# Lightning attention and a leaky-ReLU feed-forward block: heads kept in memory order, k and q of a chunk in one transfer each, w_in rows loaded in two parts

## The chip, the cores and the metric

The kernel runs on one core of one Trainium2 chip. Its time is the device time in microseconds of that core. Several runs of the same program are made and the median is given; a separate execution is recorded by the hardware profiler, and all rows below come from that one execution. Five engines work side by side: PE (matrix multiplication, with PEld for its weight loads), DVE (vector), ACT (scalar), POOL and SP, which in this kernel issues nearly all DMA transfers. Each engine runs its own instructions in a fixed order and waits for others through semaphores.

## What is computed

```
q, k, v: (4, 8, 768, 64) float32      # batch, heads, sequence, head size
w_in: (512, 2048), w_out: (2048, 512) # both float64
for b in range(12):                   # blocks of 64 positions
    intra = einsum('bhic,bhjc->bhij', qb, kb) * Dmask       # lam_h ** (i - j), lower triangle
    intra = einsum('bhij,bhjd->bhid', intra, vb)
    inter = einsum('bhid,bhde->bhie', qb * lam_pow, kv_state)
    out[:, :, sl] = intra + inter
    kv_state = lam_block * kv_state + einsum('bhsd,bhse->bhde', kb * rev_pow, vb)
x = out.transpose(0, 2, 1, 3).reshape(3072, 512)            # head h is columns 64h to 64h + 63
h = x @ w_in
g = maximum(0.01 * h, h)
result = g @ w_out                                          # (3072, 512) float32
```

The feed-forward products need more accuracy than one pass of the fast matrix format gives, so the kernel splits each factor into parts.

## The kernel before

**Tiling.** The 3072 tokens are 24 chunks of 128 (six per batch element, `NCB`), each of two blocks of 64; four chunks make a group of 512 tokens. A chunk of attention handles all eight heads together. Its result goes into the tiles `xh`, `xl`, `xm` with the 512 columns of `x` on partitions, as four row blocks of 128: two heads to a block, one in the lower 64 partitions and one in the upper. The up product multiplies these by slices of `w_in` of 256 columns (eight slices `p`), each held as three parts `wh`, `wl`, `wm`; the results pass the leaky ReLU (ACT, L883) and are stored in DRAM. When all groups are up, the down product runs over them with `w_out` prepared in the meantime. The attention of later groups is worked in between the up products of earlier ones.

**A chunk of attention.** `load_kq` (L455) and `load_v` (L525) bring k, q and v with the 128 positions on partitions and eight heads side by side. `load_kq` issues two transfers for k and two for q: heads 0, 2, 4, 6 go to the first four places of the tile, heads 1, 3, 5, 7 to the last four. `transposes` (PE, L550) turns two adjacent places at a time; copies to SBUF follow (L531 on ACT or DVE, L598 for the scaled q). From chunk 8 for q and chunk 10 for k the turned form is loaded instead by many small transfers (L513, `load_subs`, 32 partitions each) and finished by DVE. `scores` (L613) makes the products of k and v for the state (`kv`) and those of k and q (`go`); DVE multiplies the latter by the decay mask (L643) and adds to the state (L650), and POOL decays it (L653). `outputs` (L658) sums `own` (scores by v) and `inter` (state by q, in two halves, with a tiny copy L682 between them on DVE or ACT that the second half waits for) in the PSUM tile `po`. L698, L706 and L724 split the result into `xh`, `xl`, `xm`.

All small products go through `quad` (L409): a 64 × 64 weight block in one of four quadrants of the PE array, chosen by the row half (which 64 partitions the factors lie in) and the column half (which 64 output partitions). `place` (L416) tells where the scores and the state of head number `h`, in memory order, lie: heads are numbered in the tile order even-then-odd there, so that output half `hi` of row block `y` is head `2y + hi`.

**Decay factors.** `factors` (L378) copies the broadcast `lam` with the even heads first into `lam_h`; `factors_k` (L382) builds an identity-like tile `eye` (L383) and scans each head's powers (L386); `factors_q` (L389) does the same for q (L391, L393). All on DVE, in this order.

**w_in.** `w_in(p)` loads a slice in two halves `h` (L787): row blocks `2h` and `2h + 1` of 128 rows and 256 columns of float64, that is 128 partitions with two pieces of 2 KB. `to_float32` (L770) makes float32 from the bits with three ACT instructions (L799, L801, L803) and two of DVE (L805, L806); `parts` (L808) makes `wh`, `wm`, `wl` (L813 to L820). Three `raw` tiles hold the loads; one of them also takes the q of chunk 3, and the `gs` tiles take k and v of chunks 2 and 3.

**Order.** A planner (`Plan`, L45) emits the instructions. For the start and most of the up phase the order is not computed but taken from a list written out by hand (`ORDER`, L266), pairs of an operation's number and its engine; negative numbers are idle fills, identity products on PE (L349). `FIRST_LOADS` (L268) gives k, q, v of chunk 0, then chunk 1, then the slice 1 of `w_in`, and so on. SP issues every load and store in that one order.

Of the kernel before, what the change touches and what calls it, by code (L numbers as in the profile page):

```python
# [239 lines left out]
def kernel(  # L240
# [92 lines left out]
    pow_q = part(HP * C2).rearrange("p (y t) -> p y t", y=HP)  # L333
    lam_b, lam_h = part(H), part(H)
    lam_p = part(HP)
# [41 lines left out]

    def factors():  # L378
        for i in range(2):
            nc.vector.tensor_copy(lam_h[:, i * HP:(i + 1) * HP], lam_b[:, i::2])  # L380

    def factors_k():  # L382
        nc.vector.tensor_tensor(eye, ident[:, 0:C2], ident[:, C2:C], op=ALU.add)  # L383
        for hi in range(2):
            for hp in range(HP):
                nc.vector.tensor_tensor_scan(decay[:, hi, hp, :], _bc(lam_h[:, 2 * hp + hi], 1, C2), eye, 0.0,  # L386
                                             op0=ALU.mult, op1=ALU.add)

    def factors_q():  # L389
        for i in range(2):  # L390
            nc.vector.tensor_copy(lam_p[HALF[i]], lam_h[HALF[i], i::2])  # L391
        for hp in range(HP):
            nc.vector.tensor_tensor_scan(pow_q[:, hp, :], _bc(lam_p[:, hp], 1, C2), _bc(zero[:, 0], 1, C2), 1.0,  # L393
                                         op0=ALU.mult, op1=ALU.add)
# [3 lines left out]
    plan.rank = -1.0  # L398
    add("DVE", 0.25, factors, [], ["lam"])
    add("DVE", 1.65, factors_k, ["lam"], ["fk", "sc"])  # L400
# [14 lines left out]

    def place(h):  # L416
        i = h // 2 + h % 2 * HP
        return i % 2, i // 2

# [25 lines left out]
    def load_pair(nm, c):  # L445
        b, n, i = of(c)
        y, (dst, keys) = (q if nm == "q" else k)[b, :, n * C:(n + 2) * C, :], pair(nm, c)

        def go():
            for z in range(2):  # L450
                nc.sync.dma_start(out=dst[:, z * HP:(z + 1) * HP].rearrange("p h s d -> p h (s d)"),
                                  in_=y[z::2].rearrange("h (p s) d -> p h (s d)", s=2))
        move(1.75, go, [], keys, issue=1.0, name=f"{nm}{c}")

    def load_kq(c):  # L455
        b, n, i = of(c)
        for src, x, nm in ((k, 0, "k"), (q, 1, "q")):
            if paired(nm, c):
                if c % 2 == 0:
                    load_pair(nm, c)  # L460
                continue
            y, (dst, key) = src[b, :, n * C:(n + 1) * C, :], spot(nm, c)

            def go(y=y, dst=dst):
                for z in range(2):
                    nc.sync.dma_start(out=dst[:, z * HP:(z + 1) * HP, :], in_=y[z::2].rearrange("h p d -> p h d"))
            if nm == "k" or c < QD:
                move(1.15, go, [], [key], issue=1.0, name=f"{nm}{c}")
# [33 lines left out]
    def load_subs(c):  # L502
        b, n, i = of(c)
        count = run(c)[1]
        for nm, src, pieces in zip("kq", (k, q), subs(c, count)):
            for sub, lo, hi, keys in pieces:
                add("DVE", 0.0, lambda: None, [], keys)
                for y in range(lo, hi):
                    for a in range(4):
                        h = y // 2 + (2 * y + a // 2) % HP * 2  # L510
                        z = src[b, h, n * C:(n + count) * C, a % 2 * C4:(a % 2 + 1) * C4]
                        o = sub[a * C4:(a + 1) * C4, y - lo, :]
                        move(0.55, lambda o=o, z=z: nc.sync.dma_start(  # L513
                                out=o.rearrange("j (m i) -> j m i", i=C4), in_=z.rearrange("(m j) i -> j m i", j=C4)),
                            keys, [f"{nm}s{y}{a}"], issue=SUBL, rank=RUNS.get(c, (4.0, 0.4))[0] + RUNS.get(c, (4.0, 0.4))[1] * (4 * y + a))
# [97 lines left out]
    def scores(c):  # L613
# [15 lines left out]
        def kv():  # L629
            for y in range(HP):  # L630
                for x in range(2):
                    for t in range(n_pu):
                        h = y // 2 + (2 * y + x) % HP * 2
                        quad(pu[t]()[:, y, :], t, tk[:, 2 * y + x, :], tv[:, h, :], x, start=y == 0)

# [22 lines left out]
    def outputs(c, between=lambda: None):  # L658
# [3 lines left out]
        def own():  # L662
            for y in range(HP):
                for hi in range(2):
                    for t in range(2):
                        h = 2 * y + hi
                        a, z = place(h)
                        quad(po[:, t, y, :], t, tv[:, h, :], sc[:, a, z, :], hi, start=y == 0)

        def inter(m):  # L670
            for y in range(HP):
                t = y % 2 ^ m
                for hi in range(2):
                    if n or t:
                        a, z = place(2 * y + hi)
                        quad(po[:, t, y, :], a, state[(2 * c + t - 1) % 4][:, z, :], qsT[:, z, tokens(t)], hi)

# [88 lines left out]

    w_in_r = moe_w_in.rearrange("(ko ki) n -> ki ko n", ki=P)
    n_raw = 0

    def to_float32(kind, p, h, dst, key, after=()):  # L770
# [13 lines left out]
        def get():  # L784
            r64 = r().bitcast(I64)
            if kind == "wi":
                nc.sync.dma_start(out=r64.rearrange("p (k f) -> p k f", k=2),  # L787
                                  in_=w_in_r[:, 2 * h:2 * h + 2, p * 2 * P:(p + 1) * 2 * P])
            else:
# [259 lines left out]
```

## Time and profile before

| What | Value |
|---|---|
| median of 3 runs | 607.87 us (606.57 to 608.01) |
| the profiled execution, device time | 605.63 us |
| its span, first to last instruction | 603.8 us, granted TensorE clock 0.999 |
| PE busy | 596.2 us (99%), 5362 instructions |
| PE weight loads busy | 491.9 us (81%) |
| DVE busy | 299.1 us (50%), 410 instructions |
| ACT busy | 209.1 us (35%), 322 instructions |
| POOL busy | 73.9 us (12%), 85 instructions |
| SP queue: packets, MB, share of 16 engines | 149648, 104.30, 59.4% |
| loads of `w_in` | 16 of 512 KB, 5.5 us from issue to landing (median) |
| loads of k into `att` | 44 of 128 KB, 4.0 us |
| loads of v into `att` | 22 of 256 KB, 4.2 us |

How to read the rows: a line of the order of time has the start in us from the span's start, the duration in us, the engine, the line of the program, the operation, what is written and read with the shapes, and the number of instructions merged into it; in brackets stands the idle time of the engine before it and what ended that. The ends of PE rows are modelled and overlap the next ones, so distances between starts are the safer measure there. Issuing a DMA is not counted as busy time. "To landing" is the time from the start of the issue to the last of the transfer's completion marks.

### The profile page before, as it was taken

How to read it: one execution, taken by the hardware profiler on the slowest of the kernel's cores; microseconds unless marked ns; L12 is line 12 of the kernel's file. 1: busy time of each engine (PE TensorE's matmuls, PEld its weight loads, DVE VectorE, ACT ScalarE, POOL GpSimd, SP SyncE). 2: the span in 40 equal slices, each digit the busy share in tenths (PEclk: the TensorE clock that was granted, in tenths of full speed). 3: DMA queues.
4: the chain of work that ended last, by engine and by line, in shares of the span. 5: the costliest groups of instructions: out<-in, count | busy, mean ns of one | idle time of the engine just before them, and what ended most of it. 6: DMA issues, size and time to landing. Idle time of an engine off the chain costs nothing.

```text
span 603.8 us, 12715 instructions
## 1 busy us (share of the span) xinstructions
PE 596.2 (99%) x5362; PEld 491.9 (81%) x5362; DVE 299.1 (50%) x410; ACT 209.1 (35%) x322; POOL 73.9 (12%) x85
## 2 busy tenths in 40 slices
PE   8899999999999999999999999999999999999997
PEld 5788888888888888887888888888888888888886
DVE  6899854450553524344267855353453543534430
ACT  3686752222434433435334421222312313214111
POOL 3332132241322031230000000000000000000000
PEclk9999999999999999999999999999999999999999
DMA  9998887598788798655975834434333333433201
GB/s 215 226 274 214 237 226 201 96 251 202 197 227 215 230 247 233 171 199 194 323 250 194 294 105 132 148 101 139 108 120 125 122 122 123 127 101 128 82 1 69
DMA packets 149993, 105.18 MB, mean 174 GB/s; under 512 B 125872, under 2 KB 126640, under 8 KB 149936
## 3 DMA queue, kind: packets, MB, share of 16 engines
q1 hardware_dynamic: 149648, 104.30, 59.4%
q8 instruction: 42, 0.69, 0.5%
q14 instruction: 15, 0.12, 0.1%
q10 hardware_dynamic: 288, 0.07, 0.0%
HBM read 68.69 MB, written 35.65 MB: 173 GB/s over the span
## 4 chain that ended last, share of the span: by engine, by line
PE 96%; DVE 2%; DMA 0%; issue 0%; ACT 0%; DVEq 0%
PE b L856 33%; PE b L922 16%; PE psc L922 11%; PE po L922 11%; PE pt L856 11%; PE pt L922 5%; PE po L410 4%; PE psc L410 3%; DMA att<-in_lam_dram 0%; PE po L550 0%; PE b L550 0%; DVE att L393 0%; DVE att L386 0%; DVE w L806 0%; DVE att L643 0%
## 5 line engine op out<-in xcount | busy, mean ns | idle before, releaser
L904 DVE SCALAR_TENSOR_TENSOR xl<-att,xh 128x1024 fp32r<-128x1024 f32 x48 | 58.7, 1222 | 125.8 <-ACT xh L903 125.8
L903 ACT ACTIVATE xh<-att 128x1024 fp32r<-128x1024 f32 x48 | 50.9, 1061 | 147.5 <-PE po L922 73.9
L856 PE MATMUL b<-xl,wl 128*128 128x512 f32 (+1 forms) x296 | 78.1, 389 | 0.1
L856 PE MATMUL b<-xm,wm 128*128 128x512 f32 (+1 forms) x296 | 77.9, 390 | 0.0
L856 PE MATMUL b<-xh,wh 128*128 128x512 f32 (+1 forms) x296 | 77.5, 389 | 0.0
L883 ACT ACTIVATE gs<-b 128x512 f32<-128x512 f32 x73 | 42.9, 597 | 95.3 <-PE b L856 85.7
L856 PEld LDWEIGHTS b<-xl,wl 128*128 128x128 f32 x296 | 54.7, 188 | 12.0 <-DVE wl L820 0.9
L856 PEld LDWEIGHTS b<-xh,wh 128*128 128x128 f32 x296 | 54.6, 188 | 11.5 <-DVE att L598 0.3
L856 PEld LDWEIGHTS b<-xm,wm 128*128 128x128 f32 x296 | 54.4, 188 | 11.3
L906 DVE SCALAR_TENSOR_TENSOR xm<-xl,xh 128x1024 fp32r<-128x1024 f32 x48 | 58.8, 1226 | 4.7
L922 PE MATMUL b<-wh,xh 128*128 128x512 f32 x144 | 56.0, 389 | 0.0
L922 PE MATMUL b<-wl,xl 128*128 128x512 f32 x144 | 56.0, 389 | 0.0
L922 PE MATMUL b<-wm,xm 128*128 128x512 f32 x144 | 56.0, 389 | 0.0
L653 POOL TENSOR_TENSOR att<-att 128x256 f32<-128x256 f32 x40 | 29.8, 745 | 112.5 <-DVE att L650 74.0
L922 PE MATMUL psc<-wm,xm 128*128 128x512 f32 (+1 forms) x100 | 38.2, 387 | 0.0
L922 PE MATMUL po<-wm,xm 128*128 128x512 f32 (+1 forms) x100 | 37.9, 384 | 0.0
L922 PE MATMUL psc<-wh,xh 128*128 128x512 f32 x96 | 37.3, 389 | 0.0
L922 PE MATMUL psc<-wl,xl 128*128 128x512 f32 x96 | 37.3, 389 | 0.0
L922 PE MATMUL po<-wh,xh 128*128 128x512 f32 x96 | 37.3, 389 | 0.0
L922 PE MATMUL po<-wl,xl 128*128 128x512 f32 x96 | 37.3, 389 | 0.0
L410 PEld LDWEIGHTS po<-att 64*64 64x64 f32 x1408 | 26.9, 134 | 10.5 <-issue 7.8
L410 PE MATMUL po<-att 64*64 64x64 f32 x1408 | 32.9, 222 | 1.8 <-issue 1.1
(103 smaller groups left out, 859.1 us busy)
## 6 DMA issues: line engine op xcount, KB each, us to landing
att<-g SPq DMA_DIRECT2D x48, 512.0 KB, 3.4
g<-gs SPq DMA_DIRECT2D x47, 512.0 KB, 3.5
raw<-in_moe_w_in_dram SPq DMA_DIRECT2D x16, 512.0 KB, 5.5
raw<-in_moe_w_out_dram SPq DMA_DIRECT2D x16, 512.0 KB, 4.5
out_dram<-gs SPq DMA_DIRECT2D x23, 256.0 KB, 2.1
att<-in_k_dram SPq DMA_DIRECT2D x44, 128.0 KB, 4.0
att<-in_v_dram SPq DMA_DIRECT2D x22, 256.0 KB, 4.2
wo<-w SPq DMA_DIRECT2D x8, 512.0 KB, 3.9
```

The source lines that it names most:

```text
L410: nc.tensor.matmul(dst[HALF[cols]], lhsT=lhsT[HALF[rows]], rhs=rhs[HALF[rows]], start=start, stop=True, skip_group_check=True)
L653: add("POOL", 0.62, lambda new=new, j=j: nc.gpsimd.tensor_tensor(state[(j + 1) % 4], new, _bc(lam_c, 2, D), op=ALU.mult), [f"st{j % 4}", " ...
L856: nc.tensor.matmul(dst, lhsT=w[z][:, kk * 2 * P + f * P:kk * 2 * P + (f + 1) * P], rhs=x[z][:, kk, toks], start=start and kk == 0, stop=kk ...
L883: add("ACT", ns, lambda b=b, r=r: nc.scalar.activation(out=r(), in_=b(), func=AF.Prelu, bias=0.0, scale=1.0, alpha=0.01), [kb], [kg], rank ...
L903: add("ACT", 1.05, lambda: nc.scalar.activation(out=h, in_=graw[j], func=AF.Copy, bias=0.0, scale=NEAR), reads, wr("h"))
L904: add("DVE", 1.215, lambda: nc.vector.scalar_tensor_tensor(l, graw[j], 1.0, h.bitcast(F32), op0=ALU.mult, op1=ALU.subtract), reads + [f"rh ...
L906: add("DVE", 1.215, lambda: nc.vector.scalar_tensor_tensor(m, l.bitcast(F32), -S, h.bitcast(F32), op0=ALU.mult, op1=ALU.add), [f"rh{j}", f ...
L922: nc.tensor.matmul(to[:, cols], lhsT=ring[j][z][:, f * T + tb * P:f * T + (tb + 1) * P], rhs=W[pp][z][:, f * d_model:(f + 1) * d_model][:, ...
```

## The change

The heads stay in memory order in the tiles of k and q, so each comes in one transfer of 256 KB instead of two of 128 KB. The scores and the state of head `2y + a` then lie in half `a`, place `y`. In `outputs`, the column half of a head is `a` for even `y` and the other one for odd `y` (`column`): in the row blocks 1 and 3 of `x` the two heads are exchanged. The rows of `w_in` are loaded so that they match: for half `h` of a slice, the lower 64 partitions take the 64-row blocks `4h` and `4h + 3`, the upper ones `4h + 1` and `4h + 2`, in two transfers of 64 partitions. `inter` visits the two row halves for each `y` instead of alternating them from `y` to `y`. The copy into `lam_h` falls away; an empty entry keeps the numbering of `ORDER`, which is unchanged. `load_subs` and `kv` take the heads by their plain numbers.

```diff
--- before.py
+++ after.py
@@ -331,7 +331,7 @@
     state = [part(HP * D).rearrange("p (y d) -> p y d", y=HP) for _ in range(4)]
     decay = part(2 * HP * C2).rearrange("p (x y t) -> p x y t", x=2, y=HP)
     pow_q = part(HP * C2).rearrange("p (y t) -> p y t", y=HP)
-    lam_b, lam_h = part(H), part(H)
+    lam_b = part(H)
     lam_p = part(HP)
     zero = part(1)
     seen_po = part(2)
@@ -375,20 +375,16 @@
         plan.slack = 0.0
 
 
-    def factors():
-        for i in range(2):
-            nc.vector.tensor_copy(lam_h[:, i * HP:(i + 1) * HP], lam_b[:, i::2])
-
     def factors_k():
         nc.vector.tensor_tensor(eye, ident[:, 0:C2], ident[:, C2:C], op=ALU.add)
         for hi in range(2):
             for hp in range(HP):
-                nc.vector.tensor_tensor_scan(decay[:, hi, hp, :], _bc(lam_h[:, 2 * hp + hi], 1, C2), eye, 0.0,
+                nc.vector.tensor_tensor_scan(decay[:, hi, hp, :], _bc(lam_b[:, 2 * hp + hi], 1, C2), eye, 0.0,
                                              op0=ALU.mult, op1=ALU.add)
 
     def factors_q():
         for i in range(2):
-            nc.vector.tensor_copy(lam_p[HALF[i]], lam_h[HALF[i], i::2])
+            nc.vector.tensor_copy(lam_p[HALF[i]], lam_b[HALF[i], i::2])
         for hp in range(HP):
             nc.vector.tensor_tensor_scan(pow_q[:, hp, :], _bc(lam_p[:, hp], 1, C2), _bc(zero[:, 0], 1, C2), 1.0,
                                          op0=ALU.mult, op1=ALU.add)
@@ -396,7 +392,7 @@
     pow_k = decay[:, :, :, C2 - 1].rearrange("p hi hp -> p hp hi")
     lam_c = pow_q[:, :, C2 - 1]
     plan.rank = -1.0
-    add("DVE", 0.25, factors, [], ["lam"])
+    add("DVE", 0.0, lambda: None, [], ["lam"])
     add("DVE", 1.65, factors_k, ["lam"], ["fk", "sc"])
     add("DVE", 1.2, factors_q, ["lam"], ["fq"])
     if LOW_PE or MIX_PE:
@@ -413,9 +409,8 @@
     def tokens(t):
         return slice(t * C2, (t + 1) * C2)
 
-    def place(h):
-        i = h // 2 + h % 2 * HP
-        return i % 2, i // 2
+    def column(h):
+        return h % 2 ^ h // 2 % 2
 
     lower = slice(0, HP)
     upper = slice(HP, 2 * HP)
@@ -447,9 +442,7 @@
         y, (dst, keys) = (q if nm == "q" else k)[b, :, n * C:(n + 2) * C, :], pair(nm, c)
 
         def go():
-            for z in range(2):
-                nc.sync.dma_start(out=dst[:, z * HP:(z + 1) * HP].rearrange("p h s d -> p h (s d)"),
-                                  in_=y[z::2].rearrange("h (p s) d -> p h (s d)", s=2))
+            nc.sync.dma_start(out=dst.rearrange("p h s d -> p h (s d)"), in_=y.rearrange("h (p s) d -> p h (s d)", s=2))
         move(1.75, go, [], keys, issue=1.0, name=f"{nm}{c}")
 
     def load_kq(c):
@@ -462,8 +455,7 @@
             y, (dst, key) = src[b, :, n * C:(n + 1) * C, :], spot(nm, c)
 
             def go(y=y, dst=dst):
-                for z in range(2):
-                    nc.sync.dma_start(out=dst[:, z * HP:(z + 1) * HP, :], in_=y[z::2].rearrange("h p d -> p h d"))
+                nc.sync.dma_start(out=dst, in_=y.rearrange("h p d -> p h d"))
             if nm == "k" or c < QD:
                 move(1.15, go, [], [key], issue=1.0, name=f"{nm}{c}")
 
@@ -507,7 +499,7 @@
                 add("DVE", 0.0, lambda: None, [], keys)
                 for y in range(lo, hi):
                     for a in range(4):
-                        h = y // 2 + (2 * y + a // 2) % HP * 2
+                        h = 2 * y + a // 2
                         z = src[b, h, n * C:(n + count) * C, a % 2 * C4:(a % 2 + 1) * C4]
                         o = sub[a * C4:(a + 1) * C4, y - lo, :]
                         move(0.55, lambda o=o, z=z: nc.sync.dma_start(
@@ -630,8 +622,8 @@
             for y in range(HP):
                 for x in range(2):
                     for t in range(n_pu):
-                        h = y // 2 + (2 * y + x) % HP * 2
-                        quad(pu[t]()[:, y, :], t, tk[:, 2 * y + x, :], tv[:, h, :], x, start=y == 0)
+                        h = 2 * y + x
+                        quad(pu[t]()[:, y, :], t, tk[:, h, :], tv[:, h, :], x, start=y == 0)
 
         if c < GOFIRST:
             add("PE", 0.47, go, [f"kT{i}", f"qT{i}"], ["psc"], kind="q")
@@ -661,19 +653,17 @@
 
         def own():
             for y in range(HP):
-                for hi in range(2):
+                for a in range(2):
                     for t in range(2):
-                        h = 2 * y + hi
-                        a, z = place(h)
-                        quad(po[:, t, y, :], t, tv[:, h, :], sc[:, a, z, :], hi, start=y == 0)
+                        h = 2 * y + a
+                        quad(po[:, t, y, :], t, tv[:, h, :], sc[:, a, y, :], column(h), start=y == 0)
 
         def inter(m):
             for y in range(HP):
-                t = y % 2 ^ m
-                for hi in range(2):
+                for a in range(2):
+                    t = a ^ m
                     if n or t:
-                        a, z = place(2 * y + hi)
-                        quad(po[:, t, y, :], a, state[(2 * c + t - 1) % 4][:, z, :], qsT[:, z, tokens(t)], hi)
+                        quad(po[:, t, y, :], a, state[(2 * c + t - 1) % 4][:, y, :], qsT[:, y, tokens(t)], column(2 * y + a))
 
         needs = [f"qsT{i}", f"st{2 * c % 4}"] + ([f"st{(2 * c - 1) % 4}"] if n else [])
         add("PE", 0.48, own, ["sc", kv_], ["po"], kind="q")
@@ -764,7 +754,7 @@
             load_v(c + 2)
 
 
-    w_in_r = moe_w_in.rearrange("(ko ki) n -> ki ko n", ki=P)
+    w_in_r = moe_w_in.rearrange("(ko ki) n -> ki ko n", ki=C2)
     n_raw = 0
 
     def to_float32(kind, p, h, dst, key, after=()):
@@ -784,8 +774,9 @@
         def get():
             r64 = r().bitcast(I64)
             if kind == "wi":
-                nc.sync.dma_start(out=r64.rearrange("p (k f) -> p k f", k=2),
-                                  in_=w_in_r[:, 2 * h:2 * h + 2, p * 2 * P:(p + 1) * 2 * P])
+                o = r64.rearrange("p (k f) -> p k f", k=2)
+                for u, rows in enumerate((slice(4 * h, 4 * h + 4, 3), slice(4 * h + 1, 4 * h + 3))):
+                    nc.sync.dma_start(out=o[HALF[u]], in_=w_in_r[:, rows, p * 2 * P:(p + 1) * 2 * P])
             else:
                 nc.sync.dma_start(out=r64, in_=moe_w_out[(2 * p + h) * P:(2 * p + h + 1) * P, :])
 
```

## The prediction

> **What bounds the kernel now.** I read the page's busy times and 40 slices first, to see which engine limits which part.
>
> ```profile
> span 603.8 us, 12715 instructions
> ...
> PE   8899999999999999999999999999999999999997
> ...
> DVE  6899854450553524344267855353453543534430
> ...
> DMA  9998887598788798655975834434333333433201
> ```
>
> PE is busy throughout and the matmuls follow each other from about 30 us on. So nothing that merely saves work on another engine can show later than that; what is left to win or lose lies in the first two or three slices, or in PE's own work. I then cut the start into stretches. The columns are the window, its length, busy time of each engine with instruction counts, clock, DMA share and GB/s.
>
> ```profile
> 4.00:12.00 8.00, 7.32 (x135) 5.33 (x134) 6.98 (x22) 1.35 (x3) 3.02 (x4) 1.00 1.11 263
> 12.00:20.00 8.00, 6.95 (x178) 4.63 (x176) 6.39 (x11) 5.73 (x11) 2.96 (x4) 1.00 0.97 224
> 20.00:28.00 8.00, 7.33 (x231) 6.27 (x230) 7.69 (x13) 5.87 (x10) 3.61 (x4) 1.00 1.02 246
> 28.00:36.00 8.00, 7.74 (x129) 7.19 (x128) 7.65 (x11) 5.47 (x9) 2.54 (x3) 1.00 1.02 285
> 36.00:44.00 8.00, 8.00 (x144) 6.48 (x143) 7.79 (x12) 7.24 (x14) 2.71 (x3) 1.00 0.98 247
> 60.00:330.00 270.00, 270.00 (x3128) 223.59 (x3122) 124.88 (x215) 103.86 (x182) 54.59 (x59) 1.00 0.76 215
> ```
>
> From 4 to 44 us the DMA share is 0.97 to 1.11: the 16 DMA engines have no free time, while later it is 0.76. The start is therefore fed by a saturated queue, and DVE (7.65 of 8) is nearly as full. The last view is the order of time, at the places where these limits reach PE.
>
> ```profile
> 3.44 0.24 DVE L380 COPY att<-att 128x4 f32<-128x4 f32 x2 [3.44 <-DMA att<-in_lam_dram]
> 3.59 0.22 DVE L383 TENSOR_TENSOR att<-att 128x64 f32<-128x64 f32 x1
> 3.85 1.57 DVE L386 TENSOR_TENSOR_SCAN att<-att 128x64 f32<-128x64 f32 x8
> ...
> 20.32 0.44 PE L550 MATMUL b<-att,raw 128*128 128x128 f32 x2 [0.28 <-DMA raw<-in_q_dram]
> ...
> 22.72 0.68 ACT L799 ACTIVATE w<-raw 128x512 f32<-128x512 f32 x1 [0.91 <-DVE wm L818]
> ...
> 23.57 0.16 ACT L682 COPY att<-po 128x2 f32<-128x2 f32 x1 [0.17 <-PE po L410]
> ...
> 26.43 0.80 ACT L801 ACTIVATE low<-raw 128x512 uint16<-128x512 uint32 x1 [0.20 <-DMA raw<-in_moe_w_in_dram]
> ```
>
> Scans wait for lam; PE waits for a q half at 20.32; ACT takes w_in pieces as they land. Landings by the trace (issue plus time to landing of each transfer): I call the w_in loads W1a (issued 6.76, landed 12.35; first used by ACT 12.37), W1b (7.91, 13.80; 13.82), W0a (16.90, 22.56; 22.72), W0b (20.79, 26.40; 26.43), W2a (27.59, 32.90; 32.97), W2b (29.38, 34.32; 36.13). Five of these six have under 0.2 us to spare.
>
> **The change part by part.**
>
> *Factors.* The two L380 copies go (3.44 to 3.68), and L383, which reads only the identity, no longer stands behind lam. The scans start at 3.44 instead of 3.85: 0.41 us for what follows on DVE, up to the first scores at 8.18. I expect PE to lose it again at 20.32, where it waits for a transfer that does not come sooner. Bounds: -0.41 to 0.
>
> *k and q in one transfer.* 48 k issues become 24 and 16 q issues 8, each about 0.5 us on SP (median 0.51). That removes 32 × 0.5 = 16 us of SP time over the attention, and v, which already goes as 256 KB, shows the new form: 0.50 us to issue. The packets stay the same 256 B ones (18.6 ns each in the trace, 1024 × 18.6 / 16 = 1.19 us of the 16 engines for 256 KB), so the saturated engines gain nothing. The cover is the backlog: in the start a transfer lands 3.3 to 6.5 us after its issue, so an earlier issue only waits longer. In the other direction, the first half of k no longer comes alone: chunk 0's halves landed at 3.98 and 4.55 and PE began transposing at 4.19; it will begin at about 4.6. The DVE work up to 7.45 hides those 0.4 us; without it they would be PE's. I take 0.
>
> *w_in in two parts.* 16 issues become 32: 16 × 0.46 = 7.3 us more of SP, less than the k and q issues give back. Each part writes 64 partitions. No row of before shows a 2 KB load into half the partitions. Bounds per 512 KB load: its 256 packets take 98 ns each on average (84 in the median), 1.57 us on 16 engines. Lower end: the same, so 0. Upper end: each half lasts as long as the whole does now, +1.57. Below zero nothing can go, since the packets and bytes stay. Two rows lie nearest. The transposed loads of L513 write 32 partitions in 128 B packets at 12.7 ns, on the straight line through the full-width 256 B and 2 KB packets (12.9): no penalty, but at 16 × 128 / 12.7 = 161 GB/s, far below the 334 GB/s of w_in packets. The v load, the only 256 KB load into SBUF, takes 1.19 us, two of them 2.38, that is +0.81. Between ends that far apart I take 0.8, by the row of the same size.
>
> Here the Trainium skill has a rule against the change. SBUF — State Buffer, Door 1: The DMA port swizzle, says 64 partitions reach only 8 of 16 ports (196 against 328 GB/s at 1 MiB), and "Can I just issue two DMAs to hit both halves?" says two halves serialize. 512 KB at its 8 × 27.2 GB/s would be 2.4 us, by estimate +0.8 per load; by the L513 row alone it would be 0 and the sum below about -0.2. No run here shows which of the two holds.
>
> *What 0.8 per load does.* The queue is first in, first out and never empty, so each load adds its 0.8 to everything behind it. W1b is 1.6 late (15.4). ACT's three conversions behind it run 1.6 late and end at 18.0 instead of 16.4; behind them waits the small copy L682 that starts at 17.55, and PE's second half of the outputs at 18.00 waits for that: 0.5. The last q of chunk 3 lands at 21.9 instead of 20.28, and PE is already waiting: 1.6. W0a is 3 × 0.8 = 2.4 late, 24.96; ACT's L799 at 22.72 moves by 2.2, the L682 at 23.57 is queued behind it, and PE's outputs at 23.78 wait: 2.2 in all. W0b is 3.2 late, 1.0 beyond the shift; ACT stands idle 1.06 us before 28.79, which takes it. W2a is 4.0 late: 36.9 against 32.97 + 2.2, so 1.7, of which ACT's 1.35 us idle before 35.55 take all but 0.4. That goes through the conversions and DVE (7.79 of 8 busy) to L820 at 44.52, for whose result PE waits at 45.79 (0.13). Sum 2.2 + 0.4 = 2.6 us. Later loads come where PE has matmuls in stock; I count 0.
>
> *Order of the quadrant matmuls.* The exchanged halves change the order in which `own` and `inter` visit the four 64 × 64 quadrants; their number stays. Column order of pairs now alternates between head pairs in `own`, and `inter` goes crosswise.
>
> ```profile
> 9.68 0.93 PE L410 MATMUL po<-att 64*64 64x64 f32 x40 [0.22 <-DVE att L643]
> 10.54 0.66 PE L550 MATMUL b<-att 128*128 128x128 f32 x4
> ...
> 109.05 0.93 PE L410 MATMUL po<-att 64*64 64x64 f32 x48
> 109.80 1.11 PE L410 MATMUL psc<-att 64*64 64x64 f32 x64
> 110.73 0.23 PE L410 MATMUL po<-att 64*64 64x64 f32 x3
> ```
>
> The 64 records from 109.80 to 110.73 go at 14.5 ns, four every 58 ns. The 48 before them take 0.75 us although `own` goes down rows first and `inter` along columns first: the pace of 58 ns per four holds across that change of order. Only where two quadrants have all the work does it cost more: the 40 records at 9.68, whose last eight use one row of quadrants, need 0.86. In the new order every four matmuls still use all four quadrants, so I take 0. Lower end 0, since four per 58 ns is the best seen; upper end one extra step of 58 ns at each of 5 changes of order in 24 chunks: 7.0 us. Nothing covers that.
>
> *Total.* 0 + 0 + 2.6 + 0 = 2.6 us on the profiled execution (605.63 us, of which the span is 603.8): 608.2. The median of the runs, 607.87, lies 2.24 above that execution; on it the forecast is 610.5 us.
>
> **The rivals.**
>
> B: the halves cost no more (L513's row). Then only the 0.41 is in play, and most of it is lost at 20.32: 0 to -0.4, so 607.7. For it: engines that share nothing visible. Against it: w_in packets run at twice the rate that row was seen at.
>
> C: the upper price, 1.57 per load. W0a is 4.7 late, W2a 7.9, which leaves 4.6 + (7.9 - 4.6 - 1.35), about 6.5 us: 614.4. For it: two halves one after the other, no overlap. Against: the later issues wait for buffers and let the queue run down.
>
> D, the other side: the queue is not the limit, SP is. By W1a four k and q issues are saved, 2 us of SP; if W1b then lands before 13.4, ACT and DVE run early, and PE gets back the 0.41 of the factors, the 0.28 at 20.32, the 1.05 it stands at 15.00 to 16.05 and the 0.24 at 23.07: 1.98 us, 605.9. For it: SP issues back to back until 15 us. Against: a DMA share of 1.11 from 4 to 12 us.
>
> E: the new quadrant order costs its upper end, 7.0 us: 614.9. Against: the trace's indifference above.
>
> **How the numbers follow.** A measurement of this kernel tells about 0.3% (1.8 us) from no change. Forecast (0.6 to 1.0 per load, +1 to +4 us, 609 to 612) 0.50, of which 0.35 over 1.8 us; B 0.27, of which 0.02 faster; C 0.10; D 0.09; E 0.04. Slower: 0.35 + 0.10 + 0.04 = 0.49; faster 0.09 + 0.02 = 0.11; the rest, 0.40, within. The range 606.9 to 613.5 leaves out D, E and half of C, 0.18.
>
> **What would show it.** W1b landing near 15.4, W0a near 25, and packets of w_in clearly over 98 ns: the price. L383 before lam's landing and the scans at 3.44: the factors. ACT L799 and L682 later at 23 to 26, and more PE idle between 18 and 26 us: the path. 48 + 64 output and score records in 1.68 us: the order is free. I am wrong if the w_in packets keep 84 to 98 ns, or if they slow and PE's matmuls still close up by 30 us as early as now.

## The result and the profile after

| | kernel before, same chip | changed kernel |
|---|---|---|
| median of 4 runs | 607.32 us (606.57 to 608.01) | 615.36 us (614.33 to 616.05) |
| ratio, 95% interval | | 1.0134 [1.0117, 1.0152], about +8.1 us |
| span of the profiled execution | 603.8 us | 613.5 us, granted clock 1.000 |

The changed kernel is slower by three times the forecast of 2.6 us, and above the range. The page of the changed kernel, its busy slices:

```profile
span 613.5 us, 12674 instructions
...
PE   8788999999999999999999999999999999999997
...
DVE  6788777152354333453256854435354353534530
...
DMA  9999887787887888864775842623424333433301
```

One slice is 15 us. The first six of PE look almost as before; tenths are too coarse for a loss of 1.3%. The windows of the changed kernel (columns as in the prediction) show it:

```profile
12.00:20.00 8.00, 5.32 (x136) 3.32 (x138) 4.48 (x9) 4.57 (x9) 2.26 (x4) 1.00 0.99 194
20.00:28.00 8.00, 6.39 (x196) 5.30 (x191) 7.62 (x12) 4.50 (x9) 3.44 (x4) 1.00 1.02 213
28.00:36.00 8.00, 7.53 (x138) 6.54 (x137) 5.90 (x13) 5.43 (x10) 1.34 (x3) 1.00 1.10 212
36.00:44.00 8.00, 6.50 (x95) 4.86 (x94) 7.01 (x10) 4.52 (x9) 3.00 (x4) 1.00 1.18 207
44.00:52.00 8.00, 6.76 (x137) 5.48 (x136) 7.08 (x10) 5.83 (x12) 1.36 (x1) 1.00 1.11 260
52.00:60.00 8.00, 7.36 (x154) 6.16 (x153) 5.11 (x9) 4.50 (x10) 0.84 (x1) 1.00 1.05 208
60.00:330.00 270.00, 268.49 (x3155) 221.47 (x3154) 126.25 (x219) 105.38 (x186) 56.47 (x62) 1.00 0.78 214
```

The two windows of the kernel before that the prediction left out:

```profile
44.00:52.00 8.00, 7.87 (x155) 6.33 (x154) 7.42 (x14) 5.15 (x11) 0.30 (x1) 1.00 0.98 269
52.00:60.00 8.00, 8.00 (x86) 6.48 (x86) 7.93 (x12) 5.32 (x9) 3.41 (x3) 1.00 0.70 171
```

Before, the queue had run down after 52 us (share 0.70 from 52 to 60) and PE was nearly full from 36 us on. After, the DMA engines are full to 60 us and PE loses time as late as there: 1.50 us of 8 between 36 and 44, 1.24 between 44 and 52, 0.64 between 52 and 60. Fewer bytes move at a larger share: 207 GB/s at 1.18 against 247 at 0.98 from 36 to 44. What PE waits for from 28 us on in the changed kernel (waiting group, what it waited for: total, times, longest in us):

```profile
PE po L542 <- DMA att<-in_k_dram: 1.7, 3, 1.1
PE b L542 <- ACT gs L874: 1.5, 1, 1.5
PE psc L406 <- DMA att<-in_v_dram: 1.1, 2, 0.6
PE pt L542 <- DMA att<-in_q_dram: 0.5, 1, 0.5
PE po L406 <- DVE att L672: 0.3, 1, 0.3
```

In the same stretch of the kernel before only the last of these stands (0.3 us, there on L682). The new ones are the transfers of k, v and q themselves, and one wait for ACT, which in turn waited for w_in. The first line is only in part the change's: waits for k of 1.0 us in two stand in a kernel that is no slower, too (experiment 2, shown under 3 and 4). The wait for ACT and the next three in order of time, with the releaser in brackets, in the changed kernel:

```profile
43.59 0.66 PE L542 MATMUL b<-att 128*128 128x128 f32 x4 [1.50 <-ACT gs L874]
45.42 0.63 PE L542 MATMUL po<-att 128*128 128x128 f32 x4 [0.25 <-DMA att<-in_k_dram]
47.36 1.09 PE L406 MATMUL psc<-att 64*64 64x64 f32 x46 [0.45 <-DMA att<-in_v_dram]
49.28 0.66 PE L542 MATMUL pt<-att 128*128 128x128 f32 x4 [0.54 <-DMA att<-in_q_dram]
```

ACT in the first 100 us of the changed kernel:

```profile
ACT low L792 <- DMA raw<-in_moe_w_in_dram: 10.8, 6, 2.4
ACT w L790 <- DMA raw<-in_moe_w_in_dram: 9.7, 5, 2.9
```

ACT stood for 20.5 us waiting for w_in, against 1.0 us in the kernel before. It is idle time of an engine with reserve, and only what passes on to PE counts: in experiment 2, which is no slower than the kernel before, ACT waits 9.4 us for w_in.

The clearest measure is a milestone: the time at which ACT begins L688, the split of a chunk's result (L698 before). Worked out from both traces, in us:

| chunk | 0 | 1 | 2 | 3 | 4 | 5 | 6 | 7 | 8 to 10 | 13 |
|---|---|---|---|---|---|---|---|---|---|---|
| before, at | 11.7 | 18.6 | 24.3 | 28.8 | 42.4 | 51.3 | 61.2 | 68.6 | | |
| after, later by | 0.03 | 1.69 | 2.73 | 3.58 | 6.41 | 7.47 | 7.98 | 9.38 | 9.38 | 9.60 |

The profiled execution of the kernel before was one of its shorter ones (605.63 us against a median of 607.32), so some 1.7 us of the 9.6 in the last column are not the change's. Most of them arise between chunks 5 and 7: the kernels of experiments 2 and 7, which are no slower than the one before, begin chunk 5 by the same measure 0.12 us earlier than it and chunk 7 later by 1.39 and 0.96. Up to chunk 5 the table can be taken as it stands: 3.6 us of the delay arise up to chunk 3, 3.9 more up to chunk 5, from 32 to 59 us, and of the 1.9 up to chunk 7 more than half is not the change's.

### The profile page after: what moved, and what is told of

Same layout as the page of the kernel before. It is cut to its first block, busy times and chain, and to the rows that moved or that the text cites. A ratio compares the mean times of both kernels' runs of the same rounds, so it can differ in the third digit from the quotient of the medians.

```text
span 613.5 us, 12674 instructions
## 1 busy us (share of the span) xinstructions
PE 598.7 (98%) x5362; PEld 492.2 (80%) x5362; DVE 298.8 (49%) x408; ACT 208.2 (34%) x322; POOL 72.5 (12%) x85
## 4 chain that ended last, share of the span: by engine, by line
PE 88%; DMA 6%; SPq 2%; ACT 2%; DVE 2%; issue 1%; DVEq 0%; ACTq 0%
PE b L847 30%; PE b L913 16%; PE psc L913 11%; PE po L913 11%; PE pt L847 9%; PE pt L913 5%; DMA raw<-in_moe_w_in_dram 4%; PE po L406 3%; PE psc L406 2%; DMA att<-in_k_dram 2%; SPq L779 1%; SPq L458 1%; SPq L520 0%; ACT low L794 0%; ACT att L523 0%
## 5 line engine op out<-in xcount | busy, mean ns | idle before, releaser
L874 ACT ACTIVATE gs<-b 128x512 f32<-128x512 f32 x73 | 42.8, 596 | 95.3 <-PE b L847 81.2
L847 PEld LDWEIGHTS b<-xh,wh 128*128 128x128 f32 x296 | 54.6, 188 | 11.7 <-DVE att L590 0.3
L645 POOL TENSOR_TENSOR att<-att 128x256 f32<-128x256 f32 x40 | 28.3, 707 | 115.0 <-DVE att L642 92.2
```

Source lines behind the costliest of these rows:

```text
L645: add("POOL", 0.62, lambda new=new, j=j: nc.gpsimd.tensor_tensor(state[(j + 1) % 4], new, _bc(lam_c, 2, D), op=ALU.mult), [f"st{j % 4}", " ...
L847: nc.tensor.matmul(dst, lhsT=w[z][:, kk * 2 * P + f * P:kk * 2 * P + (f + 1) * P], rhs=x[z][:, kk, toks], start=start and kk == 0, stop=kk ...
L874: add("ACT", ns, lambda b=b, r=r: nc.scalar.activation(out=r(), in_=b(), func=AF.Prelu, bias=0.0, scale=1.0, alpha=0.01), [kb], [kg], rank ...
```

## The experiments

The theory after the result: the half transfers slow the shared queue, at about the forecast price, and the queue stays behind much longer than I allowed. Rivals: the number of transfers (twice as many) costs, the merged k and q cost, or the quadrant order does. Each kernel was timed beside the kernel before on the same chip.

**1. The halves alone, on the kernel before.**

```diff
-                nc.sync.dma_start(out=r64.rearrange("p (k f) -> p k f", k=2), in_=w_in_r[...])
+                o, y = r64.rearrange("p (k f) -> p k f", k=2), w_in_r[...]
+                for u in HALF:
+                    nc.sync.dma_start(out=o[u], in_=y[u])
```

> The kernel before, with nothing changed but that each w_in load goes as two transfers of 64 partitions. Theory H (pieces into half of the partitions move at about two thirds of the pace, and the first-in first-out queue hands the delay on to everything behind): w_in packets of 2 KB well above 120 ns instead of 106, the time +6 to +9 us, nearly all of what the change costs. Theory M (the merged k and q transfers cost the time, since the first half of a chunk no longer comes alone and a large transfer fills the queue): within 1.5 us of before.

Measured 614.69 against 607.10 us, 1.0118 [1.0101, 1.0135]. The waits of PE in this kernel from 28 us on:

```profile
PE b L550 <- ACT gs L884: 1.7, 1, 1.7
PE po L550 <- DMA att<-in_k_dram: 1.3, 3, 0.7
PE b L550 <- DMA att<-in_q_dram: 0.6, 2, 0.5
PE psc L410 <- DMA att<-in_v_dram: 0.4, 1, 0.4
```

The first two lead the changed kernel's list as well. The halves alone give nearly the whole loss; the rest, 0.0016, is not resolved, since the intervals of the two kernels overlap.

**2. Two transfers of full width.**

```diff
+                for u in range(2):
+                    nc.sync.dma_start(out=o[:, u], in_=y[:, u])
```

> The same number of w_in transfers as the run above (32 of 256 KB), but each into all 128 partitions, one 128-row block at a time. Theory H: within 1.5 us of before, packets about 106 ns. Rival N (it is the number of transfers, SP's 16 more issues of about 0.46 us and their place in the order): the same loss as with the halves, +5 us or more.

605.79 us, 0.9985 [0.9974, 0.9997]. Twice as many transfers cost nothing, and may gain a little. The rival of the number of transfers falls.

**3 and 4. The halves for the first six loads only, and for the last ten only.** They separate the walk of the prediction (W1a to W2b) from the loads that it counted at nothing.

```diff
+                for u in (HALF if p < 3 else (slice(0, P),)):     # 3
+                for u in (HALF if p > 2 else (slice(0, P),)):     # 4
```

> Half-width pieces for slices 0, 1 and 2 of w_in alone (the six loads that the prediction's sum followed), whole loads for slices 3 to 7. The prediction's step: +2.6 us, and this is all there is. Rival A (the delay also adds up over the later loads and reaches PE through k, q and v of chunks 4 to 8): +2 to +4 us here, about half of the whole.

> The counterpart: whole loads for slices 0, 1 and 2, half-width pieces for slices 3 to 7. The prediction counted 0 for these, since PE has matmuls in stock by then: within 1 us of before. Rival A: +3 us or more, and PE waits for DMA of k, q or v between 40 and 80 us.

First six: 611.95 us, 1.0068 [1.0050, 1.0086], about +4.1 us (the medians differ by 4.9). Last ten: 609.29 us, 1.0034 [1.0019, 1.0049], about +2.1 us. Both parts are larger than forecast (2.6 and 0). Together they make 6.2 us against 7.2 of all sixteen; the intervals do not tell these apart. The four runs of experiment 3 had a mean clock of 0.994 to 0.999, so its 4.1 us may hold some loss by the clock (last section); among the four the time does not follow the clock.

Where the 2.1 us of the last ten arise, their trace does not show. In the waits of PE from 28 us on it has a line that the kernel before lacks, but experiment 2, without any half and no slower, has it too; experiment 4 first, then 2:

```profile
PE po L550 <- DMA att<-in_k_dram: 1.0, 2, 0.6
```

```profile
PE po L550 <- DMA att<-in_k_dram: 1.0, 2, 0.7
```

**5. k and q in two transfers each again, in the changed kernel.**

```diff
-                nc.sync.dma_start(out=dst, in_=y.rearrange("h p d -> p h d"))
+                for z in (lower, upper):
+                    nc.sync.dma_start(out=dst[:, z, :], in_=y[z].rearrange("h p d -> p h d"))
```

> The changed kernel with k and q in two transfers each again (heads 0 to 3, then 4 to 7); exchange and half-width w_in pieces stay. Theory H: nothing that matters comes back, 613 to 616 us. Theory M': the merged transfers cost the remaining 1 us of the change (the first landing, 4.97 instead of 4.55): 613 to 614, and chunk 0 lands about 0.4 us earlier again.

615.82 against 606.84 us, 1.0150 [1.0126, 1.0174], beside 1.0134 [1.0117, 1.0152] of the changed kernel. The merge costs nothing that the times resolve; nor is it resolved whether it gains up to a microsecond. In the trace chunk 0 is done 0.41 us earlier than in the changed kernel, as theory M' had it (11.34 us); by chunk 3 all but 0.09 of that is gone. The merge alone, with the loads of the kernel before, was not tried.

**6. Only the exchanged row block in halves, in the changed kernel** (three transfers instead of two, half the bytes in halves).

```diff
+                nc.sync.dma_start(out=o[:, 0], in_=moe_w_in[2 * h * P:(2 * h + 1) * P, cols])
+                for u in range(2):
+                    nc.sync.dma_start(out=o[HALF[u], 1], in_=w_in_r[:, 4 * h + 3 - u, cols])
```

> The changed kernel with half-width pieces only where the exchange needs them: of the two 64-row pairs in each w_in load, the even row block goes as one transfer of 128 partitions, the odd one as two of 64 (three transfers in place of two). Half the bytes at the slow pace. Theory H: about half of the loss, +3 to +5 us against before. Rival N (number of transfers): 48 instead of 32, at least the loss of the changed kernel, +8 us.

612.30 us, 1.0081 [1.0053, 1.0110], some 4.9 us: with half the bytes in halves the loss is smaller and not larger, though there are more transfers. Part of the 4.9 may be the clock's, since all four runs had a mean clock of 0.994 to 0.997. This is the cheapest form of the exchange that was run, and still slower than the kernel before.

**7 and 8. The factors without their copies, on the kernel before; the same with the loads of experiment 2.**

```diff
-            nc.vector.tensor_copy(lam_h[:, i * HP:(i + 1) * HP], lam_b[:, i::2])
...
-                ... tensor_tensor_scan(decay[:, hi, hp, :], _bc(lam_h[:, 2 * hp + hi], 1, C2), eye, 0.0,
+                ... tensor_tensor_scan(decay[:, hi, hp, :], _bc(lam_b[:, head(2 * hp + hi)], 1, C2), eye, 0.0,
```

> The kernel before with the change's first part alone: no copies into lam_h, the factors are scanned from lam_b directly (heads picked by index), so the scans start 0.41 us earlier. The prediction's step: -0.41 to 0, most of it lost where PE waits for a q of chunk 3 at 20.32. Rival: the 0.41 is carried to the end, -0.4 us.

> The kernel before with w_in in two full-width transfers of 128 partitions and with the factors part. If the 0.9 us of the two full-width transfers and the factors' gain add up: -0.9 to -1.5 us against before, the fastest version of this study. If both only move the same wait: -0.9 us.

606.68 us, 1.0000 [0.9987, 1.0014], and 606.52 us, 0.9992 [0.9978, 1.0007]. In the trace of the first, chunk 0 is done 0.37 us earlier, chunks 1 and 5 still 0.12, and chunk 7 is 0.96 later: the 0.4 us are taken and lost, as forecast, though most of them before chunk 1 is done at 18.5 us and not at 20.32. The second shows no gain that is clear of the kernel before, so the small one of experiment 2 was not confirmed.

**9. Halves of every second partition**, 64 partitions each as well, but spread over all 128.

```diff
+                for u in range(2):
+                    nc.sync.dma_start(out=o[u::2], in_=y[u::2])
```

> The kernel before with each w_in load in two transfers of 64 partitions again, but of every second partition (even ones, then odd ones) instead of the lower and the upper half. Same count, same bytes, same 2 KB packets as with the halves. If what is slow is the contiguous half (it reaches half of the ways into SBUF): packets back near 103 ns and within 1.5 us of before. If what is slow is 64 partitions as such (fewer partitions to an engine, smaller transfers): packets near 135 ns and +6 to +8 us.

608.69 against 607.14 us, 1.0029 [1.0005, 1.0053]. The packets (table below) are back at the old pace: not 64 partitions as such, but a contiguous half is slow. The rows that are read from DRAM change together with the partitions in all these runs; that the source has no part in it was not tried by itself. The rest, 1.8 us by the ratio, is a little more than the 1.5 that I allowed. In the trace PE waits 2.03 us for ACT at 40.01, behind a w_in load that was issued later and landed at 37.46 instead of 34.32; the clock after it is taken up in the last section.

**10. No exchange: the changed kernel with whole `w_in` loads, every even head in the lower half.**

```diff
     def column(h):
-        return h % 2 ^ h // 2 % 2
+        return h % 2
```

> The changed kernel without the exchange: head 2y + a always in column half a, and so w_in again in whole loads of 512 KB. k and q in one transfer and the factors stay. Theory H: the w_in loss is gone; instead inter runs on two quadrants only, 8 steps of 58 ns in place of 4 in each of its two halves, 48 x 0.233 = 11.2 us of PE, so +10 to +12 us against before. If inter takes no longer, the exchange bought nothing and this version is the one to keep, about -0.5 us.

615.53 us, 1.0139 [1.0100, 1.0178], about +8.4 us and less than the 10 to 12 that I expected. Here the loss is of another kind. The small products of a steady chunk in this kernel, then in the changed one:

```profile
112.30 1.08 PE L406 MATMUL po<-att 64*64 64x64 f32 x45
...
113.27 1.12 PE L406 MATMUL psc<-att 64*64 64x64 f32 x62
114.21 0.65 PE L406 MATMUL po<-att 64*64 64x64 f32 x16
```

```profile
97.14 0.93 PE L406 MATMUL po<-att 64*64 64x64 f32 x48
97.89 1.11 PE L406 MATMUL psc<-att 64*64 64x64 f32 x64
98.82 0.41 PE L406 MATMUL po<-att 64*64 64x64 f32 x16
```

The 16 products of one half of `inter` are shown at 0.65 us instead of 0.41: without the exchange they use two quadrants at a time and take eight steps of 58 ns instead of four. Some 0.23 us for each of two halves in each chunk is the growth of 0.4 to 0.5 us a chunk that the milestones of this kernel show from chunk 7 on. So with heads in memory order the exchange buys on PE about as much as its halves cost on the queue.

**11 and 12. The two halves in two queues**, the upper one issued by POOL (11) or by ACT (12), in the changed kernel.

```diff
-                    nc.sync.dma_start(out=o[HALF[u]], ...)
+                    (nc.sync, nc.gpsimd)[u].dma_start(out=o[HALF[u]], ...)     # 12: nc.scalar
```

> The changed kernel with the lower 64 partitions of each w_in load issued by SP as now and the upper 64 by POOL, so that the two halves stand in two queues at once. Theory (one half in flight has only half the paths into SBUF; two halves in the air at once could share them all): the 2 KB packets of w_in go from a median of 132 ns back towards 84 ns wherever both halves overlap, W1b lands before 15.5 us instead of 17.06, and the time falls by at least 3 us to 608-612. Rival (the Trainium skill, SBUF - State Buffer, 'Can I just issue two DMAs to hit both halves?': two halves serialize, and another issuing engine does not help): packets stay at 125-140 ns, time 613-617. If POOL's own issue is what decides, its halves land clearly behind SP's and the time is above 617.

> The same with ACT issuing the upper halves instead of POOL: it tells apart the queue from the engine that issues. If two queues let the halves overlap, packets near 84-105 ns here too; ACT then loses the time of 16 issues, about 16 x 0.5 = 8 us spread over 80 us, of which it has 20% to spare in the start, so 608-613. If the halves serialize whatever the queue, packets 125-140 ns and 614-619.

619.97 and 623.33 against 607.07 us, 1.0205 [1.0175, 1.0235] and 1.0277 [1.0244, 1.0309]. With ACT issuing, the packets of SP's halves have a median of 138 ns and those of ACT's 132; POOL's halves come as packets of 4 KB at 274.5, and SP's beside them at 115.5. Two queues do not bring the 84 ns of whole loads back. The Trainium skill (SBUF — State Buffer, "Can I just issue two DMAs to hit both halves?") says that two halves serialize and that another issuing engine doesn't help; these times agree. What remains to explain is the further loss beside the changed kernel, 4.6 and 8.0 us by the medians. POOL in the first 100 us of kernel 11:

```profile
POOL raw L779 <- ACT low L794: 12.6, 5, 7.1
```

The issue of the upper half waits up to 7.1 us in POOL's order for its buffer, and POOL's decay of the state stands behind it. In kernel 12 PE waits once 6.4 us for ACT (L874). Both kernels also run at a mean clock of 0.985 to 0.989: in each trace the clock is half for two stretches of 6.83 us, which is worth up to 6.8 us of PE's work. How much of the further loss goes to the waits behind the issuing engine and how much to the clock, these runs do not separate. My expectation for 12 (614 to 619 if the halves serialize) charged only the time of the issues, neither what stands behind them nor the clock.

**The packets**, worked out from the DMA records of each trace: mean time of one packet up to 103 us, in ns; in brackets the median.

| kernel | 2 KB, w_in | 256 B, k, q, v | 256 B packets over 40 ns |
|---|---|---|---|
| before | 106 (84) | 19.0 (18) | 81 of 31744 |
| changed | 139 (132) | 22.9 (18) | 1249 of 28672 |
| 1, halves | 135 (133) | 22.2 (18) | 1054 of 28672 |
| 2, two full ones | 103 (84) | 18.9 (18) | 86 of 31744 |
| 9, every second partition | 104 (84) | 18.5 (18) | 57 of 30359 |

## Why the prediction was wrong

**The price per load, right for the load's own packets.** Forecast +0.8 us. In the median a 2 KB packet rises from 84 to 133 ns in experiment 1: 256 × 49 / 16 = 0.78 us per load. In the mean, which is what adds up, it rises from 106 to 135 over all sixteen loads, 0.46 us, and from 99.7 to 144.1 in the first six of the changed kernel, 0.71 us. These packets decide against the row of L513, and rival B falls. The Trainium skill (SBUF — State Buffer, Door 1: The DMA port swizzle) counts the ports that the partitions reach: by its table 64 neighbouring partitions reach 8 of 16, and by its formula every second partition reaches all 16. Experiments 1 and 9 agree with both (133 and 84 ns in the median).

**What the price left out: the neighbours.** I charged only the packets of w_in. The 256 B packets of k, q and v that share the queue slow down too, and only beside contiguous halves (table). For the first six loads of the changed kernel the own packets make 1536 × 44.4 / 16 = 4.26 us, and the 18112 small packets up to then go from 19.6 to 22.4 ns, 18112 × 2.8 / 16 = 3.17 us: together 7.43 us or 1.24 per load, where 0.8 was forecast. In experiment 3 the same sum gives about 1.1. For the walk to W2b the prediction had 2.6 us at 0.8 and 6.5 at 1.57; experiment 3 with 4.1 us lies between. The landings say the same: W1b at 17.06 us instead of the forecast 15.4, W0a at 25.64 where I had 25, but W0b at 31.08 and W2a at 38.73 against 26.40 and 32.90 before. By then each was 4.7 and 5.8 us late, where I had counted 3.2 and 4.0.

**The failed steps.** Two terms of the sum were too small, each by a path that it left out.

*The end of the walk: 0.4 for slice 2.* The prediction let ACT's idle time before 35.55 take up most of what W2a is late, and followed the rest through DVE to L820. The ACT row at 35.55 reads W2b, though, not W2a: its wait for the completion of W2b ended at 34.34, right behind the landing at 34.32. (I had put the first use of W2b at 36.13.) Even at 0.8 per load W2b would have landed at 39.1 and moved that row by 3.6 us, where I charged 2.6 in all. Behind the row, in ACT's fixed order, stands the copy L883 out of the PSUM tile `b`, which PE's next transposes wait for. In experiment 1:

```profile
41.10 0.67 ACT L800 ACTIVATE w<-raw 128x512 f32<-128x512 f32 x1 [1.28 <-DMA raw<-in_moe_w_in_dram]
...
42.93 0.57 ACT L884 ACTIVATE gs<-b 128x512 f32<-128x512 f32 x1
...
43.55 0.86 PE L550 MATMUL b<-att 128*128 128x128 f32 x4 [1.69 <-ACT gs L884]
```

In the changed kernel W2b lands at 41.04 us, 6.7 late, and the transposes that began at 38.34 before begin at 43.59: 5.25 us late, 1.50 of them by this wait. The same wait stands in experiment 3 (1.08 us at 43.26) and not in experiment 4, where slices 0 to 2 come whole. So the walk cost 4.1 us [3.0, 5.2] and not 2.6.

*The later loads: 0.* The prediction put it: "Later loads come where PE has matmuls in stock; I count 0." Experiment 4 shows +2.1 us [1.2, 3.0] from these loads alone, when the queue was not late before. The stock was real, but only for the up products. The attention of later chunks stands in PE's fixed order between them, and its k, q and v come through the same queue as the late w_in loads; a matmul in stock behind a waiting transpose does not run. From 28 us on PE waits 2.3 us for k, q and v when all sixteen loads go in halves (experiment 1) and 0.4 when only the first six do (experiment 3). What I had not asked is how much time these transfers had to spare. In the kernel before the k, v and q that PE waits for between 45 and 50 us in the changed one landed at 39.00, 40.42 and 41.24 us, and PE used them at 39.70, 40.98 and 42.25: 0.6 to 1.0 us. In the changed kernel they land 6.3, 6.8 and 8.0 us later. Which wait makes up the 2.1 us when the last ten loads alone go in halves stays open (experiments 3 and 4).

**The path in the first 30 us, right in kind.** I named ACT's conversions and the tiny copy behind them. In the changed kernel:

```profile
17.14 0.79 ACT L792 ACTIVATE low<-raw 128x512 uint16<-128x512 uint32 x1 [2.18 <-DMA raw<-in_moe_w_in_dram]
...
25.75 0.67 ACT L790 ACTIVATE w<-raw 128x512 f32<-128x512 f32 x1 [2.18 <-DMA raw<-in_moe_w_in_dram]
26.32 0.14 ACT L672 COPY att<-po 128x2 f32<-128x2 f32 x1
```

The copy stood at 23.57 before and stands at 26.32, 2.75 us later, where 2.2 was forecast; chunk 2's milestone is later by 2.73.

**Factors and the merge of k and q: 0 and 0, right, but not as forecast.** I expected the scans at 3.44. DVE in the changed kernel, then in experiment 5, where k and q go in two transfers each:

```profile
1.34 0.23 DVE L379 TENSOR_TENSOR att<-att 128x64 f32<-128x64 f32 x1 [1.34 <-POOL att L352]
3.89 1.57 DVE L382 TENSOR_TENSOR_SCAN att<-att 128x64 f32<-128x64 f32 x8 [2.33 <-DMA att<-in_lam_dram]
```

```profile
3.52 1.57 DVE L382 TENSOR_TENSOR_SCAN att<-att 128x64 f32<-128x64 f32 x8 [1.96 <-DMA att<-in_lam_dram]
```

The first row builds the identity, now ahead of lam; the scans wait for lam alone. In the changed kernel lam lands at 3.79 instead of 3.42, so they begin no earlier than before (3.85). It is the one transfer of k that delays lam: lam lands at 3.40 to 3.42 in the kernel before and in experiments 5, 7 and 8, where k comes in two, and at 3.78 or 3.79 in the changed kernel and in experiment 10, where it comes in one. So the merge takes back at once what the factors gain. Chunk 0 is done at 11.71 us before, at 11.34 in experiments 5 and 7, and at 11.75 in the changed kernel. I had the later first landing of k (4.97 us, its halves before at 3.98 and 4.55) hidden under DVE's work, and did not see that it moves this work itself. In the time neither effect shows by itself (experiments 5 and 7), so the two zeros do not hang on this. Neither saving SP's issues nor giving them back changed the time measurably, which speaks against rival D: the backlog on the DMA engines, not SP, sets the landings.

**Quadrant order: 0, right.** 48 + 64 records from 97.14 to 98.82 take 1.68 us, the number announced. Rival E falls. The times of rivals E (614.9) and C (614.4) lie nearest to the result, but not by their mechanisms: the quadrants keep their pace, and a load's own packets do not cost 1.57 us more.

## What to carry to other kernels

A transfer that writes a contiguous half of the partitions cost more here than its own bytes: in the full queue the small packets beside it slowed down too (22.9 against 19.0 ns), so price the queue, not the load. Where a queue is first in, first out, as it was here (in the kernel before and in the changed one the loads on SP's queue land in the order of their issue up to 110 us), a delay in one stream is a delay of all streams behind it. An engine with work in stock is covered only if none of the operations between that work waits for the same queue, so list for each transfer what it has to spare. And check which transfer an operation reads before you let an idle time in front of it take up a delay. Look for the point at which the queue runs down (here after 52 us before, after 60 us in the changed kernel), and count the loss up to there.

## What the runs showed that was not expected

**Small packets slow down beside the halves.** The 256 B packets over 40 ns go from 81 to 1249, and the mean from 19.0 to 22.9 ns. In experiment 3 it comes back to 18.1 ns after 45 us, when no half loads follow, as in the kernel before there. The Trainium skill (DMA: Bandwidth & Descriptors, Back-pressure in remote DMA) says for transfers between cores that a saturated SBUF port clogs the path back to the DMA engines and that stalled writes hold up an engine's other queues. The slower packets here are plain loads from DRAM in the same queue, so no run shows that case; that a port is the cause here was not measured by itself.

**An issue can hold its engine for 5 us.** SP's issue of k of chunk 3 lasted 5.12 us in the changed kernel (from 11.44 us on); in the kernel before the longest of the four issues of k of chunks 2 and 3 took 2.16 us, the median of its k and q issues is 0.51. The one semaphore that the issue waits for had its count at 9.72 us, when k of chunk 1 landed. That the full queue holds it is therefore likely, but inferred.

**One idle stretch can halve the clock.** PE in the profiled execution of experiment 9, first the wait, then windows of 2 us around it (the third number from the end is the granted clock):

```profile
40.01 1.03 PE L550 MATMUL b<-att 128*128 128x128 f32 x4 [2.03 <-ACT gs L884]
```

```profile
38.00:40.00 2.00, 0.00 (x0) 0.00 (x0) 1.00 (x3) 2.00 (x5) 0.62 (x1) 1.00 1.02 271
40.00:42.00 2.00, 1.99 (x7) 1.80 (x8) 0.73 (x2) 1.67 (x3) 0.00 (x0) 0.53 0.95 209
42.00:44.00 2.00, 2.00 (x37) 1.37 (x39) 1.93 (x4) 1.07 (x2) 0.32 (x1) 0.61 0.90 294
44.00:46.00 2.00, 2.00 (x101) 1.93 (x93) 2.00 (x2) 1.17 (x3) 0.74 (x1) 1.00 0.38 125
```

After 2.03 us of idle PE the clock is half for 3.41 us by the trace's clock records (0.53 and 0.61 in two windows), worth 1.7 us of PE's work. In experiment 1 a wait of 1.69 us that ended at 43.5 did the same, in experiment 6 one of 2.6 us at 64 and in experiment 3 one of 1.2 us at 22, yet waits of 2.18 and 2.17 us in experiments 3 and 6 and the changed kernel's 1.50 did not. Length alone does not decide. The Trainium skill (TensorE: Matmul & The Clock Gate, What's actually happening) has a free-running window of about 3.4 us that the activity is counted in, and puts the lower clock behind at least one idle window. The length of the drop agrees; the idle time does not, since 1.2 to 2.6 us were enough here. The position of a wait within such a window might explain which waits count, and no run here tested that. Of the ten runs of experiment 9, the four at a mean clock of 0.996 or 0.997 have a median of 610.8 us and the other six 608.2, so of the 1.5 us by which the medians differ some 0.5 go to the clock and 1.1 to other causes; the late w_in load before 40.01 is one that the trace shows, and no run isolates it. The changed kernel lost nothing to it in its profiled execution (clock 1.000), and its one run at 0.997 took 616.05 us beside 615.36 in the median.
